# Keys' first half loaded behind the first queries, and the first unit's maxima taken half by half

## The chip, the core and the metric

The kernel runs on one core of a Trainium2 chip. A core has a matrix engine (TensorE, PE in the profile), a vector engine (VectorE, DVE), a scalar engine (ScalarE, ACT), a general engine (GpSimd, POOL) and a queue that only issues transfers (SyncE, SP). Each runs its own instructions in order and waits for the others by semaphores. TensorE multiplies from SBUF into PSUM; transfers between SBUF and the chip's memory are done by 16 DMA engines. The metric is the time on the device in microseconds (us); three runs of a kernel give a median.

## What is computed

One input x (2048 rows, 448 features) goes through two attentions with 16 heads of 28 features each. Branch A looks at 8 rows only (a dilated window), branch B at all 2048. A gate from x mixes them.

```
g = sigmoid((x * gate_w).sum(-1))
a = A(x)    # q,k,v = x @ wqkv; softmax over 8 rows; @ wo
b = B(x)    # scores = q k^T * 28**-0.5; softmax over 2048 keys; @ wo
out = g * a + (1 - g) * b
```

The change concerns branch B: its projection to queries and keys, and the maximum over the keys that its softmax subtracts.

## The kernel before

Each float is kept as a high part rounded to a faster format and a low part with the rest; a product of two floats is three matrix products of parts (11 per projected tile, list ORDER, over the 448 features in four pieces, since the last piece holds the high and the low of its 64 features above each other).

The first stage projects x. It is a list of 92 tiles, numbered n: tiles 0 to 27 give queries and keys of branch B (128 features by a block of 512 rows of x, blocks nb 0 to 3), then come the values and branch A. The keys of the first group of four heads come from tile 0 (rows of x 0 to 511), tile 3 (512 to 1023), tile 6 and tile 7 (1024 to 2047); the first block of queries comes from tile 1. Tiles 0 to 9 (n < FULL) use the whole array, `project`. From tile 10 on `project_halves` splits every product over the features in two of 64 rows: one stream for array rows 0 to 63, one for 64 to 127, which are issued in turns. One of the 11 products is done by one half alone, by the block of x, so that a tile has 11 products in one half and 10 in the other: the upper half has 11 for blocks 2 and 3, the lower for blocks 0 and 1. Tiles 10 and 11 are both block 3, then pairs of blocks (0, 2) and (1, 3) follow.

ScalarE takes a tile out of PSUM (`qk_tile`, line 348 for the first ten tiles, line 353 for halves, which GpSimd adds in line 355), rounds it to the high part (line 358), VectorE or GpSimd takes the difference (349, 359), and `qk_store` sends both to memory, qk_hi and qk_lo. From there the queries and keys come back in the layout of the attention: `load_qhi` (four transfers to tiles QP) and `load_k` (four transfers to a tile KH), one for each head. SyncE issues all of these, in the order of the program. It waits in that order too: behind a store that is not ready, everything stands. A transfer also reuses the completion semaphore of the one eight places before it, and waits for it.

Beside the tiles from 11 on, the first pass over the scores runs in TensorE's halves: for unit u (a group of four heads and a block of 512 queries; 16 units) 64 products of 128 queries by 512 keys, four in each tile (`s1_half`, `s1_mm`, line 142, two for each half of the array, into banks PM). VectorE takes the maximum over the 512 keys of two products at once (line 164) into columns of the tile MX. Unit 0 covers tiles 11 to 26. When a unit's 64 columns are there, `max_parts` reduces them to 16 (four heads by four groups of 128 queries, line 176); the result is stored for the second pass. `s1_mm` numbers a product i by query group, then key quarter, then head:

```
qs, kc, h = i // 16, i // 4 % 4, i % 4
```

So tile 11 needs keys 0 to 511, tile 12 the next quarter, tile 13 the third, tile 14 the fourth, tile 15 the first again. The loads stand in the main loop over the tiles, behind the tile's products and its store: `load_qhi(0)` at n = 3, the first half of the keys (columns 0 to 1023) at n = 5, the second half at n = 8:

```
if n in (5, 8):
    load_k(0, KH[0], qk_hi, slice(0, 1024) if n == 5 else slice(1024, S))
```

After the tiles comes the attention stage: 16 units of 16 steps with the second pass of scores (line 979), exponentials on ScalarE (984), products with the values (945) and the rest of the first pass (142, 148), while GpSimd computes branch A by a plan of steps. At the end of a unit ScalarE copies the accumulator out (`fin_copy`, line 850). Then the output projection (line 832) ends the kernel.

Of the kernel before, what the change touches and what calls it, by code (L numbers as in the profile page):

```python
# [11 lines left out]
ALU = mybir.AluOpType  # L12
X = mybir.AxisListType.X
ET = mybir.EngineType

S, D, H, DH = 2048, 448, 16, 28
# [5 lines left out]
NMX = 192  # L22
# [3 lines left out]
def gated_mix_kernel(ctx: ExitStack, tc: tile.TileContext, xT, xn, gw, wA, wB, woAB, out):  # L26
    nc = tc.nc
# [3 lines left out]
    qk_hi = dram.tile([2 * D, S], F32R, name="qk_hi")  # L31
# [39 lines left out]
    KH = [cp.tile([128, S], F32R, name=f"KH{i}") for i in range(2)]  # L71
    KL = [cp.tile([128, S], F32R, name="KL0")]
    MX = cp.tile([128, NMX], F32, name="MX")
# [24 lines left out]
    def dma_r(dst, src):  # L98
        nc.sync.dma_start(dst.bitcast(F32), src.bitcast(F32))  # L99


    def load_k(g, t, src, c=slice(0, S)):
        for h in range(4):
            r = D + 112 * g + DH * h
            dma_r(t[32 * h:32 * h + DH, c], src[r:r + DH, c])
# [23 lines left out]
    def load_qhi(u):  # L129
        g, b = divmod(u, NB)  # L130
        qhis[u] = QP[u % 2]
        for h in range(4):
            r = 112 * g + DH * h
            dma_r(qhis[u][h % 2][32 * h:32 * h + DH, :], qk_hi[r:r + DH, 512 * b:512 * b + 512])

    def s1_mm(n, bank, half=False):
        u, i = divmod(n, 64)
        qs, kc, h = i // 16, i // 4 % 4, i % 4
        if i == 0 and u + 1 < NU:
            load_qhi(u + 1)  # L140
        r = slice(64 * (h // 2), 64 * (h // 2) + 64) if half else slice(32 * h, 32 * h + DH)
        nc.tensor.matmul(bank, qhis[u][h % 2][r, 128 * qs:128 * qs + 128],  # L142
                         KH[u // NB % 3][r, 512 * kc:512 * kc + 512], start=True, stop=True)
# [29 lines left out]

    def max_parts(u, later=None):
        m = sp.tile([128, 16], F32, name="m")
        nc.vector.tensor_reduce(m.rearrange("p (h q) -> p q h", h=4),
                                MX[:, 64 * u % NMX:64 * u % NMX + 64].rearrange("p (q k h) -> p q h k", q=4, h=4),
                                axis=X, op=ALU.max)
        t = sp.tile([128, 32], F32R, name="nmt")
        v = sp.tile([128, 16], F32, name="nmv")  # L180
        nc.scalar.activation(t[:, 0:16], m, AF.Copy, scale=-1.0)
        nc.scalar.activation(v, m, AF.Copy, scale=-1.0)
        low = lambda: nc.gpsimd.tensor_tensor(out=t[:, 16:32], in0=v, in1=t[:, 0:16].bitcast(F32), op=ALU.subtract)
        if later:
            later(low)
        else:
            low()
        return t
# [6 lines left out]
    def max_store(u, r):  # L195
        for a in range(4):
            nc.sync.dma_start(nm[u].bitcast(F32)[:, 32 * a:32 * a + 32], r[32 * a:32 * a + 32, :])
# [14 lines left out]
    with tc.tile_pool(name="xp", bufs=1) as xp, tc.tile_pool(name="wp", bufs=2) as wp:  # L212
# [28 lines left out]
        def split_x(nb):  # L241
            r, t = xst[:, nb, 0:3, :], xst[:, nb, 3, :]
            for kt in range(3):
                split(xh[nb][:, kt, :], xl[nb][:, kt, :], r[:, kt, :])
            tail = xh[nb][:, 3, :]
            nc.scalar.activation(tail, t, AF.Copy)
            o = LOW[nb]
            nc.vector.tensor_tensor(out=tail[o], in0=t[o], in1=tail[o].bitcast(F32), op=ALU.subtract)
# [3 lines left out]
        def load_w(wi, tails=(False, True)):  # L252
            src, cols = WSRC[wi]
            if wi not in wraw:
                wraw[wi] = raw3(), wp.tile([128, 450], F32, tag="wt", name="wt"), sum(c1 - c0 for c0, c1 in cols) + 2 * (wi == GATE)
            r, t, _ = wraw[wi]
            for tail in tails:
                o = 0
                for c0, c1 in cols:
                    e = o + c1 - c0  # L260
                    if tail:
                        both(t[:, o:e], src[384:448, c0:c1])
                    else:
                        nc.sync.dma_start(r[:, :, o:e], src[0:384, c0:c1].rearrange("(k p) c -> p k c", p=128))
                    o = e

                if wi == GATE:
                    if tail:
                        both(t[:, o:o + 2], gw[0:2, 384:448].rearrange("i p -> p i"))
                    else:  # L270
                        for kt in range(3):
                            nc.sync.dma_start(r[:, kt, o:o + 2],
                                              gw[0:2, 128 * kt:128 * kt + 128].rearrange("i p -> p i"))

        def split_w(wi, kts):
            if wi not in wsets:
                wsets[wi] = [wp.tile([128, 4, 450], F32R, tag=g, name=f"{g}{wi}") for g in ("wh", "wl")]
            wh, wl = wsets[wi]
            r, t, n = wraw[wi]
            for kt in kts:  # L280
                split(wh[:, kt, :n], wl[:, kt, :n], r[:, kt, :n] if kt < 3 else t[:, :n], nc.gpsimd)
# [24 lines left out]
        def project(n):  # L306
            order = FIRST if n == 0 else ORDER
            for i, p in enumerate(order):
                product(n, p, None, i == 0, i == len(order) - 1)
                if n == 0 and i == 0:  # L310
                    warm(3)
# [109 lines left out]
        for kt in range(3):  # L421
            if kt < 2:
                nc.vector.tensor_copy(xh[0][:, kt, :], r[:, kt, :])
            nc.vector.tensor_tensor(out=xl[0][:, kt, :], in0=r[:, kt, :], in1=xh[0][:, kt, :].bitcast(F32),
                                    op=ALU.subtract)
        nc.vector.tensor_tensor(out=tail[64:128], in0=t[64:128], in1=tail[64:128].bitcast(F32), op=ALU.subtract)
        nc.vector.tensor_tensor(out=wl0[:, 3, 0:256], in0=wt0[:, 0:256], in1=wh0[:, 3, 0:256].bitcast(F32),
                                op=ALU.subtract)
# [3 lines left out]
        def split_third():  # L432
            c = slice(256, 384)
            for kt in range(3):
                split(wh0[:, kt, c], wl0[:, kt, c], wr1[:, kt, 128:256])
            split(wh0[:, 3, c], wl0[:, 3, c], wt0[:, c])
# [19 lines left out]
        for n, t in enumerate(tiles):  # L456
            wi = t[0]
            for w in loads:
                if loads[w] == n:
                    load_w(w)  # L460
            for w in splits:
                i, k = (n - splits[w][0]) * splits[w][1], splits[w][1]
                if 0 <= i < 4:
                    split_w(w, range(i, i + k))
            if n == 0:
                split_third()
            if n in (3, 5):
                split_x((n + 1) // 2)
            if n < FULL:
                project(n)  # L470
            else:
                project_halves(n, [S1_START <= m < S1_START + 80 for m in (n, n + 1)])
            if t[1] == "qk":
                qk_tile(n, t[2], t[3])
            elif t[1] == "v":
                add_halves(n, V[:, t[2], :, 0:DH])
            else:
                a_tile(n, t[2], t[3])
            if n == 0:
                split_x(1)  # L480
            while fini and fini[0][0] <= n:
                fini.pop(0)[1]()
            if n in (2, 3):
                load_w(1, (n == 3,))
            if n == 3:
                load_qhi(0)
            if n in (5, 8):
                load_k(0, KH[0], qk_hi, slice(0, 1024) if n == 5 else slice(1024, S))
            if n == 16:
                for i in (1, 2):  # L490
                    nc.sync.dma_start(a_scr[i][:, 0:NJ, :].rearrange("c j e -> c (j e)").rearrange(
                        "c (a b) -> c a b", b=NJ), omg[0:8, None, :].to_broadcast([8, 56, NJ]))
            if n == 32:
                nc.gpsimd.memset(V[:, :, :, DH:], 1.0)
            if n == 22:
                load_k(1, KH[1], qk_hi)
            if n == 62:
                load_k(0, KL[0], qk_lo)
            if parts and parts[0][0] <= n:
                _, u, t = parts.pop(0)  # L500
                max_store(u, max_turn(t))
            if finished and n < len(tiles) - 3:
                u = finished.pop(0)
                parts.append((n + 3, u, max_parts(u)))
            if n == 64:
                gate = []
                for sgn, dst in ((-1.0, g_t), (1.0, omg)):
                    e = sp.tile([128, NJ], F32, name="ez")
                    nc.scalar.activation(e, zt, AF.Exp, scale=sgn)
                    nc.gpsimd.tensor_tensor(out=e, in0=e, in1=V[:, 0, :, DH], op=ALU.add)  # L510
                    gate.append((dst, e))
            if n in (66, 68):
                nc.vector.reciprocal(*gate.pop(0))
            if n == 70:
                nc.sync.dma_start(og_scr.rearrange("(j p) -> p j", j=NJ), omg)
            if n == 76:
                load_q(0)
# [183 lines left out]
    for c in range(8):  # L701
# [20 lines left out]
        n = 0  # L722
# [320 lines left out]
    u = NU - 1  # L1043
# [30 lines left out]
```

## Time and profile before

| what | value |
|---|---|
| median of three runs | 906.94 us (906.22 to 907.09) |
| time of the profiled execution | 906.91 us |
| its span (first to last instruction) | 905.1 us |
| TensorE busy | 896.3 us, 99% |
| VectorE busy | 734.6 us, 81% |
| ScalarE busy | 646.9 us, 71% |
| GpSimd busy | 640.7 us, 71% |
| granted clock of TensorE | 1.0 |

A row of the timeline has the start in us, the length in us, the engine, the line of the kernel, the operation, what it writes and reads, and how many instructions are merged; in brackets stands the idle time before it and what ended it. SPq is SyncE issuing a transfer, which is not the transfer's own duration. A row of waits has who waited for whom: us in total, how many times, the longest.

### The profile page before, as it was taken

Reading aid. Unit: us, or ns where it says so; the run is one execution under the profiler, and the core shown is the slowest. Engines: PE = TensorE matmul, PEld = TensorE weight load, DVE = VectorE, ACT = ScalarE, POOL = GpSimd, SP = SyncE. Lnnn points to the kernel's source line nnn. Section 1 sums busy time; section 2 is a strip of 40 time slices with the busy share of each in tenths; the row PEclk is TensorE's granted clock in tenths of the full one; section 3 lists DMA queues with packets and bytes.
Section 4 is the critical chain, followed back from the end, with each engine's and each line's share of the span. In section 5 each row is a group of like instructions: output and inputs, shape, how many; then the busy total and the mean of one; then the engine's idle time right before and its main releaser. Section 6 shows DMA issues by size and latency. Waiting matters only on the chain.

```text
span 905.1 us, 20549 instructions
## 1 busy us (share of the span) xinstructions
PE 896.3 (99%) x8326; PEld 539.4 (60%) x8326; DVE 734.6 (81%) x954; ACT 646.9 (71%) x777; POOL 640.7 (71%) x507
## 2 busy tenths in 40 slices
PE   9999999999999999999999999999999999999998
PEld 6799999999954444444444444444444444334987
DVE  6488999999979999999999999999999999721220
ACT  6456434343378888988988989889889898997220
POOL 2389847464469689999999999999999689401000
PEclk9999999999999999999999999999999999999999
DMA  9876503449373241225224242352221222245781
GB/s 266 283 250 189 170 12 84 133 123 115 106 254 73 94 129 49 71 51 159 70 57 145 81 116 76 76 136 61 61 61 27 79 55 50 81 101 150 224 265 62
DMA packets 116758, 105.04 MB, mean 116 GB/s; under 512 B 77192, under 2 KB 84744, under 8 KB 115880
## 3 DMA queue, kind: packets, MB, share of 16 engines
q1 hardware_dynamic: 116520, 103.47, 41.8%
q8 instruction: 65, 1.06, 0.5%
q10 hardware_dynamic: 144, 0.26, 0.1%
q14 instruction: 29, 0.24, 0.1%
HBM read 62.72 MB, written 40.96 MB: 115 GB/s over the span
## 4 chain that ended last, share of the span: by engine, by line
PE 93%; DMA 3%; ACT 2%; SPq 1%; DVE 0%; issue 0%; ACTq 0%
PE T L979 30%; PE av L945 27%; PE r L304 15%; PE T L832 6%; PE r L299 6%; PE r L142 4%; PE T L142 4%; ACT P L984 1%; DMA V<-in_xT 1%; DMA onlo<-on_lo 1%; DMA out<-res 0%; DMA qk_hi<-qkh 0%; DMA KH<-qk_hi 0%; SPq L99 0%; ACT KH L775 0%
## 5 line engine op out<-in xcount | busy, mean ns | idle before, releaser
L984 ACT ACTIVATE P<-T 128x1024 f32<-128x1024 f32 x512 | 497.2, 1026 | 59.1 <-PE T L979 57.7
L148 DVE TENSOR_REDUCE MX<-T 128x1 f32<-128x512 f32 x470 | 442.3, 954 | 33.9 <-PE T L142 16.9
L945 PE MATMUL av<-P,V 128*32 128x512 f32 x2048 | 272.7, 605 | 0.9 <-ACT osb L850 0.9
L979 PEld LDWEIGHTS T<-QH,KH 30*128 30x128 f32 x1024 | 92.9, 181 | 231.7 <-ACT P L984 198.3
L142 PE MATMUL T<-KH,QP 28*128 28x512 f32 x704 | 220.0, 456 | 0.1
L979 PE MATMUL T<-QH,KH 30*128 30x512 f32 x1024 | 214.1, 489 | 0.2 <-ACT P L984 0.2
L164 DVE TENSOR_REDUCE MX<-r 128x2 f32<-128x1024 f32 x160 | 192.2, 1221 | 25.7 <-PE r L142 23.9
L979 PE MATMUL T<-QH,KL 28*128 28x512 f32 x1024 | 187.7, 395 | 0.0
L979 PE MATMUL T<-QL,KH 28*128 28x512 f32 x1024 | 186.1, 393 | 0.0
L609 POOL TENSOR_TENSOR prod<-qt,kt 128x896 f32<-128x896 f32 x64 | 135.4, 2115 | 4.7 <-DMA kt<-a_scr 4.6
L367 ACT ACTIVATE raw<-r 128x896 f32<-128x896 f32 (+1 forms) x64 | 58.9, 921 | 97.5 <-PE r L304 95.3
L670 POOL TENSOR_TENSOR oat<-oat,prod 128x896 f32<-128x896 f32 x48 | 101.3, 2111 | 2.0
L142 PEld LDWEIGHTS T<-KH,QP 28*128 28x128 f32 x704 | 86.0, 181 | 27.4 <-ACT P L984 18.7
L368 POOL TENSOR_TENSOR ast<-raw 128x448 f32<-128x448 f32 x48 | 55.4, 1155 | 58.5 <-ACT raw L367 49.0
L665 POOL TENSOR_TENSOR prod<-vt,L 128x896 f32<-128x896 f32 x56 | 95.4, 1704 | 0.2
L979 PEld LDWEIGHTS T<-QL,KH 28*128 28x128 f32 x1024 | 94.3, 184 | 0.0
L979 PEld LDWEIGHTS T<-QH,KL 28*128 28x128 f32 x1024 | 93.9, 183 | 0.7
L945 PEld LDWEIGHTS av<-P,V 128*32 128x32 f32 x2048 | 40.3, 108 | 78.4 <-issue 65.2
L304 PE MATMUL r<-wh,xh 64*128 64x448 f32 (+1 forms) x512 | 82.4, 363 | 0.0
L142 PE MATMUL r<-KH,QP 64*128 64x512 f32 x320 | 80.6, 393 | 1.4 <-DMA KH<-qk_hi 1.2
L304 PE MATMUL r<-wh,xl 64*128 64x448 f32 (+1 forms) x384 | 70.1, 364 | 0.0
L614 POOL TENSOR_TENSOR prod<-prod 128x448 f32<-128x448 f32 x64 | 65.6, 1026 | 5.0
(112 smaller groups left out, 1077.6 us busy)
## 6 DMA issues: line engine op xcount, KB each, us to landing
a_scr<-ast SPq DMA_DIRECT2D x24, 448.0 KB
qk_hi<-qkh SPq DMA_DIRECT2D x24, 256.0 KB
qk_lo<-qkh SPq DMA_DIRECT2D x24, 256.0 KB
rbc<-rs SPq DMA_DIRECT2D x64, 64.0 KB
QP<-qk_hi SPq DMA_DIRECT2D x64, 56.0 KB
KL<-qk_lo SPq DMA_DIRECT2D x16, 224.0 KB
QH<-qk_hi SPq DMA_DIRECT2D x64, 56.0 KB
QL<-qk_lo SPq DMA_DIRECT2D x64, 56.0 KB
```

The costliest lines, as they stand in the source:

```text
L142: nc.tensor.matmul(bank, qhis[u][h % 2][r, 128 * qs:128 * qs + 128], KH[u // NB % 3][r, 512 * kc:512 * kc + 512], start=True, stop=True)
L148: i = nc.vector.tensor_reduce(MX[:, n % NMX:n % NMX + k], bank, axis=X, op=ALU.max)
L164: nc.vector.tensor_reduce(m, PM[k], axis=X, op=ALU.max)
L304: nc.tensor.matmul(bank[:, 0:cols], x, ws[c][rows, k, 0:cols], start=first, stop=last)
L367: nc.scalar.activation(raw[:, :, 0:cols], PJ[n % 2][:, :, 0:cols], AF.Copy)
L609: nc.gpsimd.tensor_tensor(out=p, in0=qt[c], in1=kvt["k", c % 2][:, HALO - DIL * w:HALO - DIL * w + NJ, :], op=ALU.mult)
L614: nc.gpsimd.tensor_tensor(out=lo, in0=lo, in1=hi, op=ALU.add)
L665: nc.gpsimd.tensor_tensor(out=dst.rearrange("p j (h d) -> p j h d", d=DH), in0=kvt["v", c % 2][:, HALO - DIL * w:HALO - DIL * w + NJ, :].r ...
L670: nc.gpsimd.tensor_tensor(out=ows[c % 2][:, :, 0:56] if w == W - 1 else oat[c], in0=oat[c], in1=oat[c, w], op=ALU.add)
L945: nc.tensor.matmul(av[32 * h:32 * h + 32, :], V[:, kt, 4 * g + h, :], tiles_[h], start=(kt == 0), stop=(kt == NJ - 1), skip_group_check=True)
L979: nc.tensor.matmul(bank[a], (KH[g % 3], KH[g % 3], KL[g % 2])[t][r, ks], (qh, ql, qh)[t][r, :], start=(t == 0), stop=(t == 2))
L984: e = nc.scalar.activation(p, one if a == "2" else mine, AF.Exp, scale=SCALE).ins
```

## The change

The first half of the keys is loaded at n = 3 instead of n = 5, right behind the first queries. The products of unit 0 are numbered anew: the keys' first half (two quarters) for all four query groups, then the second half. Since the columns of MX now hold the halves of the keys 32 apart, `max_parts` first takes the larger of the two, in place, for unit 0 alone, and then reduces 32 columns instead of 64. Nothing else differs.

```
     def s1_mm(n, bank, half=False):
         u, i = divmod(n, 64)
         qs, kc, h = i // 16, i // 4 % 4, i % 4
+        if u == 0:
+            qs, kc = i // 8 % 4, 2 * (i // 32) + i // 4 % 2
...
     def max_parts(u, later=None):
         m = sp.tile([128, 16], F32, name="m")
+        mx = MX[:, 64 * u % NMX:64 * u % NMX + 64]
+        if u == 0:
+            nc.vector.tensor_tensor(out=mx[:, 0:32], in0=mx[:, 0:32], in1=mx[:, 32:64], op=ALU.max)
+            mx = mx[:, 0:32]
         nc.vector.tensor_reduce(m.rearrange("p (h q) -> p q h", h=4),
-                                MX[:, 64 * u % NMX:64 * u % NMX + 64].rearrange("p (q k h) -> p q h k", q=4, h=4),
-                                axis=X, op=ALU.max)
+                                mx.rearrange("p (q k h) -> p q h k", q=4, h=4), axis=X, op=ALU.max)
...
             if n == 3:
                 load_qhi(0)
-            if n in (5, 8):
-                load_k(0, KH[0], qk_hi, slice(0, 1024) if n == 5 else slice(1024, S))
+            if n in (3, 8):
+                load_k(0, KH[0], qk_hi, slice(0, 1024) if n == 3 else slice(1024, S))
```

## The prediction

> **What bounds the kernel now.** I read the engine table first, then the chain that ended last, then the list of what TensorE waited for.
>
> ```profile
> span 905.1 us, 20549 instructions
> ...
> PE 896.3 (99%) x8326; PEld 539.4 (60%) x8326; DVE 734.6 (81%) x954; ACT 646.9 (71%) x777; POOL 640.7 (71%) x507
> ```
>
> ```profile
> 35.40 3.82 DMA qk_hi<-qkh
> 40.54 3.75 DMA KH<-qk_hi
> ```
>
> ```profile
> PE r L142 <- DMA KH<-qk_hi: 1.2, 2, 1.0
> PE av L945 <- ACT osb L850: 0.9, 1, 0.9
> ```
>
> TensorE is busy for 99% of the span and never long without work, so a microsecond is won only where it stands still or where the chain leaves it. The chain leaves it once in the region of this change: it goes through one store of projected keys (35.40) and the load of keys behind it (40.54). The waits agree: two stops of line 142, the score products of the first pass, for the tile KH. Those rows add up to 1.2 us, but a stop of one half of the array also unbalances the halves, so I read the loss from where the tiles begin:
>
> ```profile
> 33.48 1.20 PE L299 MATMUL r<-xh,wh 64*128 64x512 f32 x8
> ...
> 36.80 0.46 PE L142 MATMUL r<-KH,QP 64*128 64x512 f32 x1 [0.27 <-DMA KH<-qk_hi]
> ...
> 37.47 0.46 PE L142 MATMUL r<-KH,QP 64*128 64x512 f32 x1
> ...
> 44.43 0.59 PE L142 MATMUL r<-KH,QP 64*128 64x512 f32 x2 [0.95 <-DMA KH<-qk_hi]
> ...
> 46.95 0.73 PE L299 MATMUL r<-xh,wh 64*128 64x512 f32 x4
> ...
> 81.72 0.77 PE L299 MATMUL r<-xh,wh 64*128 64x512 f32 x4
> ```
>
> Tile 10 begins at 33.48, tile 14 at 46.95, tile 26 at 81.72. Twelve undisturbed tiles take 34.77 us, 2.898 each. Two such tiles give each half of the array (rows 0 to 63, rows 64 to 127) 25 products, so a product takes 2 x 2.898 / 25 = 0.2318 us. ORDER, its one dropped product and the inserted maxima give tiles 10 to 13 in the upper half 11 + 13 + 12 + 13 = 49 products and in the lower half 10 + 12 + 13 + 12 = 47. Without stops tile 14 would begin at 33.48 + 49 x 0.2318 = 44.84. It begins at 46.95: 2.11 us are lost. The first score product of the upper half should come after 13 products, at 36.49, and comes at 37.47: 0.98 of the loss is the first stop, and 1.13 the second.
>
> **The loads of keys, part by part.** SyncE's own queue shows why the keys are late:
>
> ```profile
> 28.22 1.85 SPq L99 DMA_DIRECT2D QP<-qk_hi  x4
> 30.17 0.35 SPq L99 DMA_DIRECT2D qk_hi<-qkh  x1
> ...
> 31.57 0.41 SPq L99 DMA_DIRECT2D qk_lo<-qkh  x1
> 32.07 2.23 SPq L99 DMA_DIRECT2D KH<-qk_hi  x4
> 34.40 0.44 SPq L99 DMA_DIRECT2D qk_hi<-qkh  x1
> ...
> 39.30 1.62 SPq L99 DMA_DIRECT2D KH<-qk_hi  x4
> ```
>
> First half of the keys. Before, four stores (tiles 4 and 5) stand between the queries and these four loads. The change swaps the two groups: the loads are issued from about 30.1 to 32.3, the stores from 32.3 to 34.3, and the store at 34.40 (tile 6) comes when it came before. From the first issue to the product that they release, the loads took 36.80 - 32.07 = 4.73 us for the lower half and 37.47 - 32.07 = 5.40 for the upper. With the same delays they are there at 34.8 and 35.5. They are wanted after 12 and 13 products, at 36.26 and 36.49. So the first stop goes, with 1.0 us to spare at the worse end. The other end is a faster landing, since the queue is then emptier:
>
> ```profile
> q1 hardware_dynamic: 294, 0.21, 32.0%
> ```
>
> ```profile
> q1 hardware_dynamic: 365, 0.68, 102.8%
> ```
>
> These are the DMA shares of 28 to 30 us and of 32 to 34 us. A faster landing would gain nothing more.
>
> The Trainium skill, "DMA: Bandwidth & Descriptors", section "Queues, rings and completion order", says that each DMA engine consumes a queue's descriptors in ring order. By that rule part of the 4.73 us was the 1 MB of stores ahead in the rings, and the loads land earlier than I count; the trace of before shows them only behind stores, so it cannot separate this. By rule or by row the sum is the same, and only the spare time differs. The same page, section "Two DMAs through the same engine are not ordered", speaks against the move: a load that reads what a store wrote must be held at the issuing engine until the store has landed, and here the whole queue would be held with it. The row bears on that: the store of tile 7's keys took 3.82 us; tile 3's, issued at 24.00, would by that be down at 27.8, 2.3 us before the load's turn, so I count nothing.
>
> Second half of the keys. Its loads stay where they are, behind the stores of tile 7. What changes is the need: unit 0 now takes keys 0 to 1023 for all four groups of queries (32 products, 8 tiles) before the first product on keys 1024 to 2047. That one moves from tile 13 to tile 19, which without stops begins at 44.84 + 5 x 2.898 = 59.3. The second half released TensorE at 44.43; even a further delay of several us is covered. The second stop goes, -1.13.
>
> The delayed stores. Stores of tiles 4 and 5 go out 2.1 to 2.2 us later. By the program's waits, their buffers are next written by ScalarE's rounding of tile 10, behind the eviction of tile 11 (about 40, by the products counted above), and by the eviction of tile 12 (about 42). At 3.82 us for a store they are down by 38. Stores 6 and 7 reuse the completion semaphores of the moved loads; with landings at 34.8 to 35.5 that can hold them up by 0.5 us, which only delays the second half of the keys. I count 0; the other bound is again 0.5 on work that has 14 us of cover.
>
> The reordered products. The order permutes which slices line 142 reads; number, shapes and banks are the same: 0.
>
> The extra maximum. One VectorE instruction on 128x32 values is added, once, and the reduction after it reads 32 columns instead of 64. Its nearest rows:
>
> ```profile
> 84.38 1.23 DVE L164 TENSOR_REDUCE MX<-r 128x2 f32<-128x1024 f32 x1 [0.40 <-PE r L142]
> 85.64 0.27 DVE L176 TENSOR_REDUCE m<-MX 128x16 f32<-128x64 f32 x1
> 85.83 1.20 DVE L164 TENSOR_REDUCE MX<-r 128x2 f32<-128x1024 f32 x1
> 87.26 2.47 DVE L164 TENSOR_REDUCE MX<-r 128x2 f32<-128x1024 f32 x2 [0.22 <-PE r L142]
> 93.69 0.20 DVE L192 STREAM_TRANSPOSE nms<-nmt 128x32 f32<-128x32 f32 x1
> ```
>
> Between 0 and 0.27 us; I take 0.2, the row with as many elements. Behind it VectorE's next maxima wait, and TensorE waits for those only when it rewrites their bank. The maximum of 85.83 ends at 87.03, the next product into that bank comes at about 87.9, and VectorE idles 0.22 us before each pair. Hidden: 0. With that cover gone it would cost 0.2.
>
> **Sum.** -0.98 - 1.13 = -2.11 us. Both ends: -1.2, if only the idle time in the waits is won, and -2.58, if the lower half's 47 products set tile 14 (44.37). I take 2.11, since the next stage needs both halves. The profiled execution took 906.91 us around its span of 905.1 us: it should become 904.8, span 903.0. The median of 906.94 is the same within 0.03, so the forecast is 904.8. Behind tile 14 everything is released by TensorE or by what follows from it, so the shift should last:
>
> ```profile
> 46.95:87.30 40.35, 40.35 (x352) 40.35 (x349) 34.24 (x30) 23.89 (x35) 36.85 (x33) 1.00 0.75 217
> ...
> 253.00:830.00 577.00, 575.76 (x5837) 238.49 (x5837) 509.39 (x725) 516.08 (x582) 487.24 (x349) 1.00 0.33 91
> ```
>
> The columns are length, then busy time of TensorE, its weight loads, VectorE, ScalarE and GpSimd, clock, DMA share, GB/s. TensorE has no gap in the first stretch and 1.24 us in the long one.
>
> **Rivals.** One: the first stop stays. The first half lands past 36.5 after all, because the loads are held in SyncE's queue for an earlier store. Then only 1.13 is won: 905.8. Against it is the spare of 1.0 us.
>
> Two: the gain is given back to GpSimd. In the first of these stretches it is busy 36.85 of 40.35 us, and TensorE's stops gave it time to catch up. The tight place, as ScalarE, GpSimd and TensorE show it:
>
> ```profile
> 88.09 0.64 ACT L358 ACTIVATE qkh<-raw 128x512 fp32r<-128x512 f32 x1 [2.14 <-POOL raw L355]
> ...
> 88.84 1.01 ACT L353 ACTIVATE raw<-r 128x1024 f32<-128x1024 f32 x1
> ```
>
> ```profile
> 48.37 1.29 POOL L355 TENSOR_TENSOR raw<-raw 128x512 f32<-128x512 f32 x1 [1.69 <-ACT raw L353]
> ...
> 59.97 1.29 POOL L355 TENSOR_TENSOR raw<-raw 128x512 f32<-128x512 f32 x1 [0.35 <-ACT raw L353]
> ```
>
> ```profile
> 90.17 0.64 PE L304 MATMUL r<-wh,xh 64*128 64x448 f32 x4
> ```
>
> Tile 27's eviction waits behind GpSimd and ends at 89.85; tile 29 overwrites its banks at 90.17, only 0.32 us later. Were GpSimd all of 2.11 us later there relative to TensorE, TensorE would lose 2.11 - 0.32 = 1.79: 906.6. Against it: at 59.97 GpSimd still idles 0.35 us in a tile because ScalarE has nothing for it. It has caught up long before 88, and does so without the stops too.
>
> Three, slower: the hand-over at the end of a unit in the attention stage. There the first product into the accumulator waits for ScalarE to copy it out (line 850), once, for 0.9 us, out of 15 such copies. A stage that begins 2.11 us earlier meets its transfers in another phase. If k copies more are waited for, the time is 904.8 + 0.9 k: from three on it is slower than before (907.5), and five, a third of them, make the 909.3 that I price it at. For it is only that one such wait exists; against it that program order and releases there are unchanged.
>
> **How the numbers follow.** What a measurement here tells from no change is about 0.2%, 1.8 us: faster is below 905.1, slower above 908.8. All of the forecast: 0.72, its own range 904.2 to 905.5. Rival one: 0.10. Rival two, in whole or in part (905.3 to 906.6): 0.10. Rival three, with five copies: 0.08. Nine tenths of the forecast's chance lie below 905.1 (three runs of one kernel differ by 0.87 us, and its middle is 0.3 below that bound): faster 0.66. Same takes the other tenth of it, rivals one and two, and a share of three with fewer copies: 0.27. Slower keeps 0.07 of rival three. The range reaches from 904.0 (a gain of 2.58 with some scatter) to 906.3, which takes in rival one and most of rival two.
>
> **What would show it.** In the profile of the changed kernel TensorE has no wait for KH; the four loads of the first half are issued directly behind those of QP, near 30 us; tile 14 begins at 44.8 and the twelve tiles behind it still take 34.8 us; the second half lands at 44 to 45 with nobody waiting; one new VectorE row of about 0.2 us stands ahead of m; GpSimd's 0.35 us gaps are there before 66 us. The prediction is wrong if the first product of the upper half comes later than 36.5, if tile 14 begins on time but the first products of the attention stage do not come 2.1 us earlier, or if new waits stand in the attention stage.

## The result, and the profile after

The changed kernel takes 912.21 us (median of 6 runs, 911.91 to 912.93) against 906.59 us for the kernel before (6 runs beside it): a ratio of 1.0061, interval 1.0050 to 1.0073. It is 5.6 us slower. Forecast were 904.8 us, 2.1 us faster.

What TensorE waited for, in the profile of the changed kernel (lines from 142 on have moved down by 2 to 6):

```profile
PE r L144 <- DVE MX L166: 4.9, 1, 4.9
PE r L214 <- DVE omg L210: 1.4, 1, 1.4
PE av L950 <- ACT osb L855: 0.9, 1, 0.9
```

The two stops for KH are gone. In their place stands one stop of 4.9 us, for a maximum of VectorE. TensorE's timeline shows both, the gain and the loss:

```profile
33.90 1.20 PE L304 MATMUL r<-xh,wh 64*128 64x512 f32 x8
...
36.77 0.39 PE L144 MATMUL r<-KH,QP 64*128 64x512 f32 x1
...
37.02 0.39 PE L144 MATMUL r<-KH,QP 64*128 64x512 f32 x1
...
44.22 0.61 PE L144 MATMUL r<-KH,QP 64*128 64x512 f32 x2
...
91.46 0.80 PE L144 MATMUL r<-KH,QP 64*128 64x512 f32 x2 [4.93 <-DVE MX L166]
```

The same two places in the kernel before, the last pair of score products of tile 13 and the first pair of tile 28:

```profile
46.14 0.51 PE L142 MATMUL r<-KH,QP 64*128 64x512 f32 x2
...
87.94 0.53 PE L142 MATMUL r<-KH,QP 64*128 64x512 f32 x2
```

In the changed kernel tile 10 begins at 33.90, and the last pair of score products of tile 13 comes at 44.22, 10.32 us later. Before, that pair stood 12.66 us behind the start of tile 10. So 2.34 us are won there (forecast 2.11). The first products of the two halves come 2.87 and 3.12 us behind the start of tile 10; forecast were 2.78 and 3.01. SyncE's queue is in the order that the change asks for:

```profile
28.32 1.85 SPq L99 DMA_DIRECT2D QP<-qk_hi  x4
30.27 1.61 SPq L99 DMA_DIRECT2D KH<-qk_hi  x4
31.98 0.35 SPq L99 DMA_DIRECT2D qk_hi<-qkh  x1
...
39.45 1.64 SPq L99 DMA_DIRECT2D KH<-qk_hi  x4
```

The loss is 40 us further on, at the end of unit 0. VectorE's timeline there:

```profile
83.94 6.11 DVE L180 TENSOR_TENSOR MX<-MX 128x32 f32<-128x32 f32 x1
90.08 0.19 DVE L182 TENSOR_REDUCE m<-MX 128x16 f32<-128x32 f32 x1
90.19 3.48 DVE L166 TENSOR_REDUCE MX<-r 128x2 f32<-128x1024 f32 x3
```

The one added operation, 32 columns, lasts 6.11 us instead of 0.2. GpSimd at that time:

```profile
82.95 1.20 POOL L226 TENSOR_TENSOR wl<-raw,wh 128x448 fp32r<-128x448 f32 x1
84.07 1.03 POOL L226 TENSOR_TENSOR wl<-wt,wh 128x448 fp32r<-128x448 f32 x1
85.00 1.34 POOL L360 TENSOR_TENSOR raw<-raw 128x512 f32<-128x512 f32 x1
86.25 1.32 POOL L364 TENSOR_TENSOR qkh<-raw,qkh 128x512 fp32r<-128x512 f32 x1
87.47 1.31 POOL L360 TENSOR_TENSOR raw<-raw 128x512 f32<-128x512 f32 x1
88.69 1.31 POOL L364 TENSOR_TENSOR qkh<-raw,qkh 128x512 fp32r<-128x512 f32 x1
90.71 0.22 POOL L188 TENSOR_TENSOR nmt<-nmv,nmt 128x16 fp32r<-128x16 f32 x1 [0.71 <-ACT nmv L187]
```

GpSimd works without a break until 90.00; VectorE's operation ends at 90.05. GpSimd falls idle there for a reason that leads back to VectorE: its next instruction (90.71) waits for nmv, ScalarE makes nmv from m, and VectorE makes m behind the added operation. ScalarE's row shows that wait:

```profile
90.31 0.22 ACT L186 ACTIVATE nmt<-m 128x16 fp32r<-128x16 f32 x1 [3.30 <-DVE m L182]
```

And the stop costs more than its own length. These are stretches of 2 us with, among others, TensorE's busy time first and the granted clock as the third number from the end:

```profile
88.00:90.00 2.00, 0.00 (x0) 0.00 (x0) 2.00 (x1) 0.00 (x0) 2.00 (x2) 0.81 0.73 178
90.00:92.00 2.00, 0.54 (x2) 0.50 (x4) 1.97 (x4) 1.69 (x4) 0.60 (x2) 0.50 1.01 307
...
94.00:96.00 2.00, 2.00 (x14) 1.75 (x12) 1.04 (x1) 0.00 (x0) 0.12 (x1) 0.50 0.72 266
96.00:98.00 2.00, 2.00 (x22) 1.89 (x20) 1.39 (x2) 1.44 (x2) 0.94 (x1) 0.98 0.59 211
```

From 91.46 to about 96.1 TensorE works at half its clock: 4.6 us that hold the work of 2.3. The account: the last pair of tile 13 is 1.92 us earlier than before; the first score products of tile 28, due at 86.02 (87.94 before, less 1.92), come at 91.46, 5.4 us late; the half clock takes 2.3 us. -1.92 + 5.4 + 2.3 = +5.8. The first score products of the attention stage (line 979 before, 984 after) come at 261.22 against 255.35, +5.87, and the output projection (line 832 before, 837 after) begins on the chain at 836.61 against 830.67, +5.94. So the attention stage between has given almost nothing and taken almost nothing.

### The profile page after: what moved, and what is told of

The parts are those of the page before. It is cut to its first block, busy times and chain, and to the rows that moved or that the text cites. A ratio compares the mean times of both kernels' runs of the same rounds, so it can differ in the third digit from the quotient of the medians.

```text
span 910.7 us, 20550 instructions
## 1 busy us (share of the span) xinstructions
PE 898.4 (99%) x8326; PEld 528.5 (58%) x8326; DVE 740.3 (81%) x955; ACT 646.6 (71%) x777; POOL 640.3 (70%) x507
## 4 chain that ended last, share of the span: by engine, by line
PE 94%; ACT 2%; DMA 2%; DVE 1%; SPq 1%; issue 0%; ACTq 0%
PE T L984 30%; PE av L950 27%; PE r L309 15%; PE T L837 7%; PE r L304 6%; PE r L144 4%; PE T L144 4%; ACT P L989 1%; DMA V<-in_xT 1%; DVE MX L180 1%; DMA oar<-oa_scr 1%; DVE MX L166 0%; ACT KH L780 0%; SPq L99 0%; ACT onhi L888 0%
## 5 line engine op out<-in xcount | busy, mean ns | idle before, releaser
L144 PE MATMUL r<-KH,QP 64*128 64x512 f32 x320 | 86.5, 397 | 5.0 <-DVE MX L166 4.9
```

## The experiments

Three theories. **P**: the added operation is held because both its operands lie in SBUF while GpSimd works there without a gap. **F**: the operation is slow in itself, as the first of its kind or because it works in place. **M**: the moved load or the new order costs the time and VectorE only shows it. Each kernel ran beside the kernel before on the same chip.

**The move without the operation.** The maxima of unit 0 go to the columns where the old order had them.

```
         if halves[k] == 2:
             halves[k] = 0
-            m = MX[:, n % NMX:n % NMX + 4].rearrange("p (a b) -> p a b", b=2)[:, :, k]
+            c = n % NMX
+            if n < 64:
+                c = 16 * (n // 8 % 4) + 4 * (2 * (n // 32) + n // 4 % 2)
+            m = MX[:, c:c + 4].rearrange("p (a b) -> p a b", b=2)[:, :, k]
...
-        if u == 0:
-            nc.vector.tensor_tensor(out=mx[:, 0:32], in0=mx[:, 0:32], in1=mx[:, 32:64], op=ALU.max)
-            mx = mx[:, 0:32]
```

> The changed kernel with the maxima of unit 0 written to the old columns, so that the extra VectorE operation is not needed; load and order of the products stay as changed. Theory P (the extra operation is held because it reads two SBUF operands while GpSimd works without a gap): the stop of 4.9 us and the halved clock go, the gain of the load and the order remains, 904.2 to 904.8 us. Theory F (the operation is slow in itself, by its first use or by working in place): the same. Theory M (the loss comes from the moved load or the new order, and VectorE only shows it): 910 us or more.

Measured: 904.38 us against 906.97, ratio 0.9974 (0.9964 to 0.9983). TensorE's longest waits in it:

```profile
PE r L214 <- DVE omg L210: 1.4, 1, 1.4
PE av L950 <- ACT osb L855: 0.9, 1, 0.9
```

No wait for KH, none for VectorE in the first pass. M falls. The moved load and the new order bring 2.4 us (1.5 to 3.3), and the forecast of 2.11 lies in the interval. This version is faster than both kernels.

**One reduction in place of two operations.**

```
-        if u == 0:
-            nc.vector.tensor_tensor(out=mx[:, 0:32], in0=mx[:, 0:32], in1=mx[:, 32:64], op=ALU.max)
-            mx = mx[:, 0:32]
-        nc.vector.tensor_reduce(m.rearrange("p (h q) -> p q h", h=4),
-                                mx.rearrange("p (q k h) -> p q h k", q=4, h=4), axis=X, op=ALU.max)
+        mo = m.rearrange("p (h q) -> p q h", h=4)
+        if u == 0:
+            nc.vector.tensor_reduce(mo, mx.rearrange("p (a q k h) -> p q h a k", a=2, q=4, h=4),
+                                    axis=mybir.AxisListType.XY, op=ALU.max)
+        else:
+            nc.vector.tensor_reduce(mo, mx.rearrange("p (q k h) -> p q h k", q=4, h=4), axis=X, op=ALU.max)
```

> The changed kernel with the extra operation and the reduction behind it joined into one reduction over two axes of the same 64 columns: one SBUF operand instead of two. P: 0.2 to 0.3 us for it beside a busy GpSimd, 904.2 to 905.0 us. F: the same, if only that operation is slow. M: 910 us or more.

Measured: 904.64 us against 906.97, ratio 0.9974 (0.9965 to 0.9984). The same maxima of the same 64 columns, in the same place, with one operand, take what the reduction of 64 columns took before (0.27 us), although GpSimd works there without a break:

```profile
83.14 0.27 DVE L181 TENSOR_REDUCE m<-MX 128x16 f32<-128x64 f32 x1
```

**The same operation, later.**

```
-            if finished and n < len(tiles) - 3:
+            if finished and n < len(tiles) - 3 and (finished[0] > 0 or n >= 34):
```

> The changed kernel with the extra operation, unchanged, issued some 8 tiles later, behind tile 34, where GpSimd has gaps of over a microsecond in each tile. P: it lasts until the next gap, 0.2 to 1.3 us; no stop of TensorE of over 1 us, clock 1.0, 904.3 to 905.8 us. F: 6.1 us again, with the stop and the halved clock, 911 to 913 us.

Measured: 904.46 us against 906.97, ratio 0.9969 (0.9959 to 0.9979). VectorE, then GpSimd around it:

```profile
105.08 0.18 DVE L180 TENSOR_TENSOR MX<-MX 128x32 f32<-128x32 f32 x1
```

```profile
103.99 1.19 POOL L226 TENSOR_TENSOR wl<-raw,wh 128x450 fp32r<-128x450 f32 x1
105.41 1.16 POOL L373 TENSOR_TENSOR V<-raw 128x448 f32<-128x448 f32 x1 [0.23 <-ACT raw L372]
```

GpSimd is at its end at 105.18 and next busy at 105.41; the operation runs into that gap and ends at 105.26. The operation itself, first of its kind and in place, takes 0.18 us. F falls.

**The operation alone, in the kernel before.**

```
         m = sp.tile([128, 16], F32, name="m")
+        if u == 0:
+            nc.vector.tensor_tensor(out=probe, in0=MX[:, 0:32], in1=MX[:, 32:64], op=ALU.max)
         nc.vector.tensor_reduce(m.rearrange("p (h q) -> p q h", h=4),
```

> The kernel before with nothing but the extra operation, on the same columns and at the same place behind tile 26, its result written to a tile that nothing reads. P: it lasts as long as GpSimd works without a gap, some 6 us, TensorE stops for about 5 us and the clock is halved for a while: 913.5 to 915.5 us. F by first use: the same. F by working in place: about 0.2 us, 906.6 to 907.0 us, since this one does not work in place. M: 906.6 to 907.0 us.

Measured: 913.51 us against 906.97, ratio 1.0068 (1.0051 to 1.0085). VectorE, then the end of GpSimd's work, then TensorE's wait:

```profile
85.71 6.10 DVE L178 TENSOR_TENSOR probe<-MX 128x32 f32<-128x32 f32 x1
```

```profile
90.50 1.27 POOL L362 TENSOR_TENSOR qkh<-raw,qkh 128x512 fp32r<-128x512 f32 x1
92.42 0.22 POOL L186 TENSOR_TENSOR nmt<-nmv,nmt 128x16 fp32r<-128x16 f32 x1 [0.65 <-ACT nmv L185]
```

```profile
PE r L143 <- DVE MX L165: 5.4, 2, 4.9
```

Most of the loss comes back without the load, without the new order and without working in place. Again the operation ends (91.81) with GpSimd's run (91.77), and again GpSimd's next instruction waits for what follows from m. The operation costs 6.2 us here (4.6 to 7.7); less the 2.4 us that the move brings (1.5 to 3.3), that makes a loss of 3.8 us (1.3 to 6.2, end against end), and the changed kernel shows 5.6. The traces have part of the difference: here the score products of tile 28 come 5.1 us late and TensorE then works for 3.2 us at half clock, which costs 1.6 us; in the changed kernel it is 5.4 us and 4.6 us of work at half clock, 2.3 us.

**Operands and place.** Three operations of this kind in the kernel before, on columns of a constant tile; the one behind tile 24 takes one of them from PSUM.

```
+            if n in (15, 24, 27):
+                first = PM[1][:, 1, 0:32] if n == 24 else ident[:, 0:32]
+                nc.vector.tensor_tensor(out=probe, in0=first, in1=ident[:, 32:64], op=ALU.max)
             if t[1] == "qk":
                 qk_tile(n, t[2], t[3])
```

> The kernel before with three operations of the same kind and size (maximum of two operands of 128x32, result read by nobody): behind tile 15 and behind tile 27 both operands in SBUF (columns of the identity), behind tile 24 one of them in PSUM. Theory P (two SBUF operands, held until GpSimd has a gap): tile 15, where GpSimd idles 0.35 us in each tile, 0.2 to 2.6 us; tile 24, where GpSimd works without gaps, 0.15 to 0.3 us; tile 27 until GpSimd's next gap, 3 to 6 us, with a stop of TensorE. Rival Q (any operation of two operands is held, wherever they lie): tile 24 takes 4 us or more and TensorE stops there already. Rival L (held for one GpSimd instruction at most, the 6 us having another cause): none of the three over 1.5 us. Time by P: 911 to 914 us.

Measured in a single execution: 909.05 us against 907.12, below what P had given (911 to 914). The three operations, and GpSimd around the second and the third:

```profile
53.06 0.24 DVE L476 TENSOR_TENSOR probe<-ident 128x32 f32<-128x32 f32 x1
...
79.13 0.18 DVE L476 TENSOR_TENSOR probe<-r,ident 128x32 f32<-128x32 f32 x1
...
87.86 3.40 DVE L476 TENSOR_TENSOR probe<-ident 128x32 f32<-128x32 f32 x1
```

```profile
78.08 1.33 POOL L360 TENSOR_TENSOR qkh<-raw,qkh 128x512 fp32r<-128x512 f32 x1
79.33 2.33 POOL L222 TENSOR_TENSOR wl<-raw,wh 128x448 fp32r<-128x448 f32 x2
...
87.38 1.36 POOL L360 TENSOR_TENSOR qkh<-raw,qkh 128x512 fp32r<-128x512 f32 x1
88.62 1.35 POOL L356 TENSOR_TENSOR raw<-raw 128x512 f32<-128x512 f32 x1
89.88 1.33 POOL L360 TENSOR_TENSOR qkh<-raw,qkh 128x512 fp32r<-128x512 f32 x1
91.11 0.28 POOL L184 TENSOR_TENSOR nmt<-nmv,nmt 128x16 fp32r<-128x16 f32 x1
```

Behind tile 15 the operation takes 0.24 us and ends (53.30) as GpSimd reaches a gap of 0.35 us (it is busy until 53.26), as P says. With one operand in PSUM the operation takes 0.18 us although GpSimd works without a break around it: rival Q falls. With both in SBUF it takes 3.40 us behind tile 27, through the rest of one GpSimd instruction and two whole ones: rival L falls too. But it ends at 91.26, at the hand-over to the short instruction of line 184, where the profile shows no gap; P said a gap. TensorE stopped for 2.2 us here, and its clock stayed at 1.0 in all of the run. A shorter stop without a half clock fits a time below P's.

**A relieved GpSimd.** The changed kernel with its added operation, without eight of GpSimd's subtractions ahead of it.

```
+                raw = r[:, kt, :n] if kt < 3 else t[:, :n]
+                if wi in (2, 3):
+                    nc.scalar.activation(wh[:, kt, :n], raw, AF.Copy)
+                    nc.scalar.activation(wl[:, kt, :n], raw, AF.Copy)
+                else:
+                    split(wh[:, kt, :n], wl[:, kt, :n], raw, nc.gpsimd)
```

> The changed kernel, extra operation and all, with GpSimd relieved ahead of it: the low parts of the weights of sets 2 and 3 (eight subtractions on GpSimd between tiles 20 and 25) are replaced by copies of the whole weights on ScalarE, so the low parts that enter the products are wrong and the output differs; number and shapes of the products are the same. Theory P: GpSimd then idles 0.35 us in each tile behind tile 26 too, the operation ends in the next such gap, 0.2 to 2.6 us, TensorE stops for at most 1.5 us, the clock stays at 1.0, 904.2 to 906.0 us. If the length of the operation has nothing to do with GpSimd's gaps: 6.1 us again, a stop of 4.9 us and 911 to 913 us.

Measured: 906.00 us against 906.00 on this chip, ratio 0.9988 (0.9975 to 1.0002), and none of TensorE's waits in it is for VectorE's maxima.

```profile
83.93 0.92 DVE L180 TENSOR_TENSOR MX<-MX 128x32 f32<-128x32 f32 x1
```

```profile
83.51 1.29 POOL L369 TENSOR_TENSOR qkh<-raw,qkh 128x512 fp32r<-128x512 f32 x1
84.75 1.30 POOL L365 TENSOR_TENSOR raw<-raw 128x512 f32<-128x512 f32 x1
```

The same operation at the same time, 0.92 us instead of 6.11: it ends at 84.85 with the GpSimd instruction that was running (84.80). The backlog ahead of it is what made it long. Whether this kernel keeps the whole gain of the move the interval doesn't tell; it also gives ScalarE eight more copies.

**The load alone, the order alone.** In the kernel before, the load at tile 3 only:

```
-            if n in (5, 8):
-                load_k(0, KH[0], qk_hi, slice(0, 1024) if n == 5 else slice(1024, S))
+            if n in (3, 8):
+                load_k(0, KH[0], qk_hi, slice(0, 1024) if n == 3 else slice(1024, S))
```

> The kernel before with the first half of the keys loaded at tile 3 and nothing else. The prediction's split of the gain: the first stop goes (0.98 us), the second stays, since tile 13 still needs keys 1024 to 1535 and their load is where it was, and takes back what the first gave: TensorE reaches tile 13 earlier and waits until the same 44.4 us. So 906.4 to 907.0 us, no gain. Rival: the second half also lands earlier, since less stands before it, and 905.4 to 906.0 us come out.

Measured: 907.17 us against 907.12, ratio 1.0002 (0.9991 to 1.0014).

```profile
36.35 0.39 PE L142 MATMUL r<-KH,QP 64*128 64x512 f32 x1
36.59 0.39 PE L142 MATMUL r<-KH,QP 64*128 64x512 f32 x1
...
44.23 0.59 PE L142 MATMUL r<-KH,QP 64*128 64x512 f32 x2 [1.68 <-DMA KH<-qk_hi]
```

The first stop is gone, and TensorE waits the longer at the second, for the same moment: 44.23 instead of 44.43. As expected, there is no gain; the time lies just above the expected range (906.4 to 907.0). In the profiled execution (908.85 us) the clock fell behind this stop, for some 3.4 us, which costs 1.7 us:

```profile
46.00:48.00 2.00, 2.00 (x12) 2.00 (x11) 0.60 (x2) 0.00 (x0) 0.00 (x0) 0.50 0.80 220
```

The other half is the kernel of the first experiment with the load back at tile 5:

```
-            if n in (3, 8):
-                load_k(0, KH[0], qk_hi, slice(0, 1024) if n == 3 else slice(1024, S))
+            if n in (5, 8):
+                load_k(0, KH[0], qk_hi, slice(0, 1024) if n == 5 else slice(1024, S))
```

> The kernel before with the new order of unit 0's products, written to the old columns, and the loads where they were. The first stop stays (0.98 us), the second goes: 905.3 to 906.0 us. Rival: the first stop is not worth what was counted and nearly all of the gain is here, 904.3 to 904.9 us.

Measured: 906.00 us against 907.12, ratio 0.9992 (0.9982 to 1.0001).

```profile
37.27 0.47 PE L144 MATMUL r<-KH,QP 64*128 64x512 f32 x1 [0.33 <-DMA KH<-qk_hi]
```

The first stop stays as it was (37.47 before), the second is gone: the last two score products of tile 13 come 10.90 and 11.35 us behind the start of tile 10, where it was 12.66 before. In the time the gain is 0.7 us with an interval from -0.1 to 1.6: the 1.13 us expected lie in it, and so does no gain.

## Why the prediction was wrong

The two loads. This part was right: the first half was there when it was wanted, the second half was waited for by nobody, and the stores that now go out later held up nothing that TensorE waited for. The gain was 2.34 us between tiles 10 and 13, and 2.4 us in the run without the added operation, against 2.11 forecast. One sign of being wrong did appear, a first product of the upper half later than 36.5 (37.02), but tile 10 itself began 0.42 us later in this execution; counted from there the product came at 3.12 instead of 3.01 us and had not waited. The split into 0.98 and 1.13 was right in kind: the load alone only lengthens the second stop (`load_only`), and the order alone removes it (`order_only`), though its gain in time is not clear of nothing.

The reordered products. They cost nothing, as predicted: the run without the added operation has them and keeps the gain.

The extra maximum. This is the step that failed. It said "between 0 and 0.27 us; I take 0.2, the row with as many elements", and "hidden: 0". The operation took 6.11 us and cost a stop of 4.93 and some 2.3 us at half clock. The rows I took, a reduction and a transposition, have one operand. The operation has two, both in SBUF, and stands where GpSimd is busy without a break; both were needed for the loss (`reduce`, `probes` behind tile 24, `late`, `gaps`). That the bound of 0.27 us was drawn from the wrong rows could have been seen: the kernel before has operations with two SBUF operands on VectorE in the projection (line 221), but where GpSimd is nearly idle. In a view by stretches of the kernel before, the fifth busy time is GpSimd's:

```profile
16.00:33.50 17.50, 17.30 (x76) 13.84 (x76) 10.29 (x17) 9.80 (x19) 3.39 (x4) 1.00 0.91 288
```

No row of before showed such an operation started while GpSimd was busy: the two that met GpSimd at all (at 5.11 and 859.63) had begun before it and shared 0.15 us with it at most. So the price had no bound from above in the trace. GpSimd's 36.85 busy us of 40.35 stood in the prediction, as a danger to ScalarE's evictions, not to VectorE.

A rule that I had not weighed speaks of this. The Trainium skill, "SBUF — State Buffer", sections "SBUF: two separate sides" and "Who interferes with whom", says that VectorE reads its second SBUF operand through a port that it shares with GpSimd, and that of two such instructions the later one is blocked until the first has finished. On which operations collide the traces agree: 0.18 us with one operand in PSUM, 6.10 with both in SBUF. On how long they do not: taken at its word the rule would give at most one GpSimd instruction, 1.34 us here, and the operation stood through five whole ones. By the rule alone, an estimate, the operation would have taken at most 1.34 + 0.18 us against the 0.9 us for which the prediction had seen cover (87.03 to 87.9), a loss of under a microsecond; the measurement decides.

The rivals. One, that the first stop stays, did not come. Two had the place nearly right, the end of unit 0, and the wrong mechanism. Three, the hand-over in the attention stage, did not come: that wait is 0.9 us, once, as before. The chance of 0.07 for slower was for a mechanism that had nothing to do with what happened.

## What to carry to other kernels

Price an added operation by a row with the same operands in the same places and the same neighbours at work, not by one with the same number of elements; where there is no such row, the trace gives its cost no upper bound, and another form (here the two-axis reduction, or other columns for the results) is cheaper than finding out. On VectorE, an operation with two operands in SBUF beside a backlogged GpSimd is the case to look for. And a stop of TensorE can cost more than its length, since the clock may fall with it: it did with stops of 4.9 and of 1.7 us, and did not with one of 2.2.

## What the runs showed of the hardware

The hold is not for one instruction. VectorE's operation of 0.18 us stood through the rest of one GpSimd instruction and five whole ones in the changed kernel (6.11 us) and again alone (6.10), through two whole ones behind tile 27 of the probes (3.40), and through none with GpSimd relieved (0.92). In the first two cases it ended when GpSimd had nothing to do, since GpSimd's next instruction waited for what VectorE makes behind the operation; in the last two at a hand-over between instructions without a gap in the profile, whose spans of GpSimd are rough. What opens the way at one hand-over and not at another stays open.

The clock does not go by the length of a stop alone. Read in stretches of a quarter to half a microsecond, it fell to 0.5 at 2.7 us into the stop of 4.93 us (changed kernel) and stayed there for 6.8 us; it fell at 4.7 us into the stop of 4.86 us (the operation alone) and stayed for 3.4 us; it fell 0.9 us behind the end of the stop of 1.68 us (the load alone) and stayed for 3.4 us; and the stop of 2.16 us (the probes) did not touch it. The Trainium skill, "TensorE: Matmul & The Clock Gate", section "What's actually happening", puts the limit at an idle window of about 3.4 us. The lengths of the low stretches, one or two times 3.4 us, agree with such a window; the limit does not, since 1.68 us without work were enough in one run and 2.16 us were not in another. Here the measurement decides, and what else brings the clock down stays open.
